# Products of a constant in front of the matrix products that a build-time order expects to find TensorE idle

## Chip, cores and metric

The kernel runs on one core of one Trainium2 chip. The metric is the device time of one execution in microseconds (us); three runs of the kernel before took 1369.7 to 1370.69, with a median of 1370.52.

## What is computed

Three layers follow one another. The first is attention with 2 batches, 8 heads, 576 positions and 64 columns per head, in which only the 32 largest scores of a row count. Its output, 1152 rows of 512 columns, goes through a mixture of 8 experts in which every expert sees every row and is weighted by a matrix that eight Sinkhorn sweeps balance. The result goes through a second mixture in which each row goes to its best expert, and at most 288 rows to one expert.

```python
scores = scale * np.matmul(q, k.transpose(0, 1, 3, 2))
mask = scores >= np.partition(scores, -32, axis=-1)[..., -32:-31]
attn = softmax(np.where(mask, scores, -1e9))
x = np.matmul(attn, v)                             # 1152 x 512
P = exp(x @ w_gate - max)                          # 8 sweeps over rows and columns
x2 = sum(P[:, e:e+1] * (np.maximum(x @ w1[e], 0) @ w2[e]) for e in range(8))
expert = np.argmax(x2 @ w_gate2, axis=1)           # at most 288 rows each
out[i] = gate[i] * (np.maximum(x2[i] @ w1b[e], 0) @ w2b[e])
```

## The kernel before

**Precision.** Each operand of a large product is split into a high and a low part of type fp32r (ScalarE rounds the high part, VectorE or GpSimd subtracts), and each product is three matrix products: high by high, high by low, low by high.

**The order.** The kernel does not issue instructions as its functions run. Each function describes jobs to an object of class `Order`: an engine, a rank, a cost in us, the jobs it depends on, the buffers it takes from pools and those it uses. When all is described, `run` takes, again and again, the job that can start first by these costs, and `put` calls its function, which emits its instructions. `self.t["PE"]` is the moment at which TensorE is done with what it has by this reckoning, and the start of the chosen job less that moment is the idle time that the order expects of TensorE. The order of the instructions on each engine is so fixed when the kernel is built; on the chip each engine works through its own list in that order, and waits on semaphores.

**Attention** (`keys`, `block`, `search`, `values`, L376 to L608). A block is 128 queries of one head. TensorE turns queries and keys (L214), forms the scores in two halves of 288 columns (L489) into PSUM, ScalarE copies them. VectorE finds the 32 largest in four rounds of MAX8 and MATCH_REPLACE8 (L504 to L510), masks the exponentials (L519). TensorE turns the result (L214), and after a pair's blocks multiplies it by the values in a chain of ten products (L596, here called a mix). ScalarE lifts one half of the mix (L599), and VectorE adds the other half (L601). PSUM tiles `tp` (a pool of three, `psa`) serve all of this.

**First mixture** (`mixture_one`, `late_one`, `visit`, `layer2`): products L693 and L717 into PSUM tiles `yp`, a pool of five (`psm`). The first group's attention, 16 blocks, must be done before the first of these products can start; the other groups' blocks are interleaved with them. **Sinkhorn** (L758 to L798) and the routing of rows (`route_all`, L906 to L976) follow: per tile of 128 rows, turn (L214), gate products (L928), choice on VectorE, count (L950, L951), place, and a scatter of the rows to HBM (L968).

**Second mixture** (`mixture_two`, L825 to L904). Per expert it fetches 288 rows (tile `x`) from HBM, turns them in 12 transposes of 96 rows (L214), three to a tile `tp`; ScalarE and VectorE split each tile (L851, L853), and eight units of products (L868: 12 products of 288 columns; L879: 12) follow. The transposes of the second expert come right behind those of the first, before its products. The end is the products of the last expert and the scatter of its rows (L898).

**What the change touches:** `Order.__init__`, `Order.run` (L114 to L127), `Net.build` (L218), the constant `ones_b` (L294, L295: 128 x 128 in bf16, written by GpSimd; so far used by the count alone), and the pool `psm`.

```python
s = max(self.t[j.eng], j.est)                    # Order.start: when a job could begin
...
self.t[e] = s + j.cost                           # Order.put: when its engine is done with it
...
self.psm = self.pool(ps, "yp", [128, 512], 5)    # Net.places
```

Of the kernel before, what the change touches and what calls it, by code (L numbers as in the profile page):

```python
# [36 lines left out]
class Pool:  # L37


    def __init__(self, tiles, line=True):  # L40
        self.free = [(0.0, t) for t in tiles]
        self.line, self.made, self.given = line, 0, 0
# [19 lines left out]
class Order:  # L62
# [9 lines left out]
    def __init__(self):  # L72
        self.t = {e: 0.0 for e in self.ENGINES}
        self.ready = {e: [] for e in self.ENGINES}
        self.left = 0
        self.moved = 0.0
        self.log = []

    def job(self, eng, rank, cost, fn, deps=(), take=(), use=(), est=0.0, lag=None):
# [33 lines left out]
    def run(self):  # L113
        while self.left:  # L114
            best = None
            for e in self.ENGINES:
                c = [(self.start(j), j.rank, n) for n, j in enumerate(self.ready[e])]
                c = [x for x in c if x[0] is not None]
                if not c:
                    continue  # L120
                s = min(c)[0]
                _, n = min((r, n) for t, r, n in c if t <= s + 0.02)
                if best is None or s < best[0]:
                    best = s, e, n
            assert best, "no job can start"
            self.put(*best)

    def put(self, s, e, n):
# [43 lines left out]
class Net:  # L172
# [45 lines left out]
    def build(self):  # L218
        with ExitStack() as st:
            self.st = st  # L220
            self.mem = self.space(st, "all")
            self.drams = self.space(st, "scratch", space=DRAM)
            self.places(st)
            self.constants()
            self.sa = ExitStack()
            self.places_a()
            self.attention()
            self.mixture_one()
            self.gate = self.job("X", 0, 0.0, self.turn_over, deps=self.attended)
            self.sinkhorn()  # L230
            self.late_one()
            self.mixture_two()
            self.o.run()
            self.sb.close()

    def places(self, st):
        ps = self.space(st, "psum", space=PSUM)
        self.psa = self.pool(ps, "tp", [128, 512], 3, line=False)
        self.psm = self.pool(ps, "yp", [128, 512], 5)
        w = self.mem  # L240
        self.r1 = self.pool(w, "ra", [128, 4, 128], 3)
        self.r2 = self.pool(w, "rb", [128, self.DM], 3)
        self.w1 = self.pairs(w, "w0", [128, 4, 128], 3)
        self.w2 = self.pairs(w, "w1", [128, self.DM], 4)
        self.h = self.pairs(w, "h", [128, 512], 3)
        self.ys = self.pool(w, "ys", [128, self.DM], 2)
        self.xt = [w.tile([128, 4, self.N], F32R, name=n) for n in ("xh", "xl")]
# [763 lines left out]
```

## Time and profile before

| | |
|---|---|
| time, median of 3 runs | 1370.52 us (1369.7 to 1370.69) |
| the profiled execution's own time | 1370.26 us |
| its span, first to last instruction | 1368.5 us |
| mean granted TensorE clock | 0.948 of full speed |
| TensorE busy | 1276.2 us, 93% |
| VectorE busy | 951.0 us, 69% |
| ScalarE busy | 794.5 us, 58% |
| GpSimd busy | 402.7 us, 29% |

PE is TensorE, PEld its loading of weights, DVE VectorE, ACT ScalarE, POOL GpSimd. A row of a timeline gives the start, the duration, the engine, the line of the code, the operation, output and inputs, their shapes and how many such instructions it merges; in brackets stand the idle time before it and who ended that. [...]

### The profile page before, as it was taken

The page shows a single profiled execution, that of the slowest core. Times are in us where ns is not written, and L with a number is a line of the kernel's source. Part 1 is how long each engine was busy: PE and PEld are TensorE (multiplying, and loading weights), DVE is VectorE, ACT ScalarE, POOL GpSimd, SP SyncE. Part 2 cuts the span into 40 slices and gives each one's busy share as a digit, 9 for nine tenths or more (in the row PEclk, how much of TensorE's full clock was granted, in tenths as well). Part 3 has the DMA queues.
Part 4 walks back from the last instruction along what each step waited for, and adds up shares of the span by engine and source line. Part 5 has one row for each costly group of instructions (what it writes and reads, how often), then busy time and mean ns, then how long its engine had stood idle before and what let it go on. Part 6 is the DMA issues. An engine that isn't in the chain of part 4 may idle for free. (4 is left out here: it accounts for less than half of the span.)

```text
span 1368.5 us, 22394 instructions
## 1 busy us (share of the span) xinstructions
PE 1276.2 (93%) x7315; PEld 1123.1 (82%) x7315; DVE 951.0 (69%) x2291; ACT 794.5 (58%) x1861; POOL 402.7 (29%) x414
## 2 busy tenths in 40 slices
PE   5567999999999999999979999999999978999997
PEld 3345878888899888888858888899988968999997
DVE  7998999999999999662564453555446744555652
ACT  6776878888898877433334333343334524655663
POOL 5633746787877743231000000000000010001001
PEclk9655899999999999999989999999999988999999
DMA  4500477465555523133673343444435634666661
GB/s 110 139 15 21 130 234 223 147 183 170 171 170 173 168 78 103 46 104 117 210 223 108 93 124 108 124 124 126 128 101 158 196 109 130 185 187 181 192 174 48
DMA packets 238213, 189.25 MB, mean 138 GB/s; under 512 B 44816, under 2 KB 188176, under 8 KB 238097
## 3 DMA queue, kind: packets, MB, share of 16 engines
q1 hardware_dynamic: 235840, 183.10, 45.9%
q0 software_dynamic: 2256, 4.73, 1.0%
q8 instruction: 57, 0.93, 0.3%
q14 instruction: 60, 0.48, 0.1%
HBM read 167.56 MB, written 22.57 MB: 139 GB/s over the span
## 5 line engine op out<-in xcount | busy, mean ns | idle before, releaser
L651 ACT ACTIVATE hh<-yp 128x256 fp32r<-128x256 f32 (+4 forms) x264 | 119.2, 451 | 253.8 <-PE yp L693 191.0
L653 DVE SCALAR_TENSOR_TENSOR hl<-yp,hh 128x256 fp32r<-128x256 f32 (+4 forms) x264 | 133.1, 504 | 188.8 <-ACT hh L651 188.4
L637 ACT ACTIVATE w1h<-rb 128x512 fp32r<-128x512 f32 x264 | 166.8, 632 | 155.3 <-PE yp L717 123.0
L717 PE MATMUL yp<-w1h,hh 128*128 128x512 f32 x552 | 222.8, 404 | 5.0 <-DVE acc L745 4.5
L717 PE MATMUL yp<-w1l,hh 128*128 128x512 f32 x552 | 218.1, 395 | 0.0
L717 PE MATMUL yp<-w1h,hl 128*128 128x512 f32 x552 | 217.8, 395 | 0.0
L640 DVE TENSOR_TENSOR w1l<-rb,w1h 128x512 fp32r<-128x512 f32 x160 | 110.6, 691 | 125.2 <-ACT w1h L637 125.1
L693 PE MATMUL yp<-xh,w0h 128*128 128x256 f32 (+3 forms) x832 | 175.0, 333 | 6.5 <-DVE acc L745 3.9
L693 PE MATMUL yp<-xh,w0l 128*128 128x256 f32 (+3 forms) x832 | 174.1, 331 | 0.0
L693 PE MATMUL yp<-xl,w0h 128*128 128x256 f32 (+3 forms) x832 | 173.5, 331 | 0.0
L637 ACT ACTIVATE w0h<-ra 128x512 fp32r<-128x512 f32 x272 | 169.8, 624 | 0.0
L643 POOL TENSOR_TENSOR w0l<-ra,w0h 128x512 fp32r<-128x512 f32 x104 | 134.8, 1296 | 110.9 <-ACT w0h L637 101.5
L693 PEld LDWEIGHTS yp<-xh,w0h 128*128 128x128 f32 x832 | 139.4, 191 | 28.3 <-DVE acc L745 4.6
L510 DVE MAX8 m<-wk 128x8 f32<-128x576 f32 x216 | 158.1, 745 | 0.4
L968 POOL DMA_INDIRECT disp<-acc,idx x9 | 10.1, 1118 | 488.5 <-DVE idx L964 488.5
L643 POOL TENSOR_TENSOR w1l<-rb,w1h 128x512 fp32r<-128x512 f32 x104 | 134.7, 1295 | 60.4 <-ACT w1h L637 56.5
L693 PEld LDWEIGHTS yp<-xh,w0l 128*128 128x128 f32 x832 | 135.7, 192 | 10.1 <-POOL w0l L643 0.5
L693 PEld LDWEIGHTS yp<-xl,w0h 128*128 128x128 f32 x832 | 135.8, 191 | 8.2 <-issue 0.2
L717 PEld LDWEIGHTS yp<-w1h,hl 128*128 128x128 f32 x552 | 104.3, 189 | 22.9
L717 PEld LDWEIGHTS yp<-w1h,hh 128*128 128x128 f32 x552 | 104.5, 189 | 21.7 <-DVE acc L745 4.5
L640 DVE TENSOR_TENSOR w0l<-ra,w0h 128x512 fp32r<-128x512 f32 x168 | 115.8, 689 | 5.2 <-ACT w0h L637 1.1
L717 PEld LDWEIGHTS yp<-w1l,hh 128*128 128x128 f32 x552 | 104.6, 190 | 14.0
(153 smaller groups left out, 2347.2 us busy)
## 6 DMA issues: line engine op xcount, KB each, us to landing
ra<-in_moe_w_dram SPq DMA_DIRECT2D x272, 256.0 KB, 2.9
rb<-in_moe_w_dram SPq DMA_DIRECT2D x272, 256.0 KB, 2.8
y<-ys SPq DMA_DIRECT2D x28, 256.0 KB, 3.0
disp<-z SPq DMA_DIRECT2D x1, 4626.0 KB, 16.3
x<-disp SPq DMA_DIRECT2D x8, 578.2 KB, 4.8
qg<-in_q_dram SPq DMA_DIRECT2D x64, 64.0 KB, 2.3
vr<-in_v_dram SPq DMA_DIRECT2D x32, 128.0 KB, 2.6
yt<-y SPq DMA_DIRECT2D x16, 256.0 KB, 3.6
```

The source lines that it names most:

```text
L510: j = self.job("DVE", r, 0.66, lambda i=i: nc.vector.max(m.t[:, i + 1], wk.t), deps=[j], use=[wk] if i == 2 else [])
L637: jh = self.job("ACT", -500 + rank, t_act(512, True), lambda r=r, w=w: nc.scalar.activation(w.t[0], r.t, AF.Copy), deps=[j], take=[w])
L640: jl = self.job("DVE", -100 + rank, t_dve(512, True), lambda r=r, w=w: nc.vector.tensor_sub(w.t[1], r.t, w.t[0].bitcast(F32)), deps=[jh], ...
L643: jl = self.job("POOL", -100 + rank, t_pool(512), lambda r=r, w=w: nc.gpsimd.tensor_sub(w.t[1], r.t, w.t[0].bitcast(F32)), deps=[jh], use=[r])
L651: jh = self.job("ACT", -1000 + k * 0.001, t_act(b - a), lambda: nc.scalar.activation(h.t[0][:, a:b], p.t[:, :b - a], AF.Relu), deps=deps, ...
L653: jl = self.job("DVE", -1000 + k * 0.001, t_dve(b - a), lambda: nc.vector.scalar_tensor_tensor(h.t[1][:, a:b], p.t[:, :b - a], 0.0, h.t[0] ...
L693: nc.tensor.matmul(p.t[:, :b - a], w1[0].t[i][:, d, :], self.xt[s][:, d, c0 + a:c0 + b], start=m == 0 and d == 0, stop=m == 2 and d == 3)
L717: nc.tensor.matmul(y[t].t, h.t[i][:, c:c + 128], w2[0].t[s], start=f == 0 and m == 0, stop=f == last and m == 2)
L968: i = nc.gpsimd.indirect_dma_start(out=self.disp, out_offset=bass.IndirectOffsetOnAxis(ap=v()["idx"][:, :1], axis=0), in_=x(), in_offset=N ...
```

## The change

`run` calls a hook each time the next job is one of TensorE's, with the idle time that the order expects before it. The hook, `Net.busy`, does nothing if that is under 1.0 us, or if no PSUM tile of the pool `psm` is free by the order's clock. Otherwise it emits, ahead of the job, as many products of `ones_b` by `ones_b` as fill 0.7 of the idle time at 0.23 us each. Each loads the 128 x 128 constant as weights, streams it four times (512 columns, bf16) and writes 128 x 512 into the free `yp` tile that has been free longest. Nobody reads the result: the next user of the tile starts its sum anew. The products are no jobs: the order's clock, ranks and buffers do not know of them, so the order of all other instructions stays as it was.

```diff
@@ class Order
         self.moved = 0.0
+        self.keep = None
         self.log = []
...
             assert best, "no job can start"
+            if best[1] == "PE" and self.keep:
+                self.keep(best[0] - self.t["PE"])
             self.put(*best)
@@ class Net, build
             self.st = st
+            self.o.keep = self.busy
...
+    def busy(self, idle):
+
+        free = [x for x in self.psm.free if x[0] <= self.o.t["PE"]]
+        if idle < 1.0 or not free:
+            return
+        b = self.ones_b
+        for _ in range(int(0.7 * idle / 0.23)):
+            self.nc.tensor.matmul(min(free, key=lambda x: x[0])[1], b, b[:, None, :].to_broadcast([128, 4, 128]),
+                                  start=True, stop=True)
```

## Rows read from the trace of the kernel before

**Rows 1.** The page: busy time by engine; TensorE and its granted clock in 40 slices.
```profile
PE 1276.2 (93%) x7315; PEld 1123.1 (82%) x7315; DVE 951.0 (69%) x2291; ACT 794.5 (58%) x1861; POOL 402.7 (29%) x414
...
PE   5567999999999999999979999999999978999997
...
PEclk9655899999999999999989999999999988999999
```

**Rows 2.** Busy time by stretch: length, then each engine, granted clock, DMA share, GB/s.
```profile
0.00:45.00 45.00, 26.37 (x90) 17.67 (x90) 34.26 (x90) 33.47 (x98) 24.91 (x47) 1.00 0.53 133
45.00:145.00 100.00, 65.33 (x236) 48.08 (x237) 89.00 (x242) 69.13 (x194) 43.38 (x61) 0.54 0.15 39
145.00:547.00 402.00, 394.78 (x2441) 344.48 (x2441) 395.60 (x1084) 338.38 (x866) 273.56 (x252) 0.99 0.56 166
...
1120.38:1140.86 20.48, 9.48 (x47) 8.65 (x47) 5.80 (x25) 3.68 (x10) 0.98 (x1) 0.50 0.31 78
...
1150.00:1340.00 190.00, 189.71 (x1472) 189.45 (x1471) 111.33 (x196) 111.97 (x236) 16.53 (x18) 1.00 0.64 181
```

**Rows 3.** TensorE's groups by form: scores in 0 to 42, then in 83 to 144.
```profile
L489 PE MATMUL tp<-kst,qs 128*128 128x288 f32 x30 | 10.8, 497 | 7.2 <-ACT kst L412 3.7 <-ACT sc L494 2.2 <-ACT er L552 1.1
...
L489 PE MATMUL tp<-kst,qs 128*128 128x288 f32 x29 | 10.4, 491 | 5.3 <-ACT er L552 4.8 <-ACT sc L494 0.5
```

**Rows 4.** Waits of VectorE, 45 to 145: us in total, times, longest.
```profile
DVE xr L601 <- ACT up L599: 8.1, 6, 2.3
```

**Rows 5.** Timeline of TensorE: the last mix of the first group; a mix later on.
```profile
133.68 0.58 PE L596 MATMUL tp<-eth,vs 128*128 128x256 f32 x1 [0.50 <-ACT sc L494]
...
136.07 0.41 PE L596 MATMUL tp<-etl,vs 64*128 64x256 f32 x1
...
330.88 0.28 PE L596 MATMUL tp<-eth,vs 128*128 128x256 f32 x1
...
332.14 0.28 PE L596 MATMUL tp<-etl,vs 64*128 64x256 f32 x1
```

**Rows 6.** Timeline of TensorE: neighbouring products of 512 columns, at 193 and at 704.
```profile
193.23 0.39 PE L717 MATMUL yp<-w1l,hh 128*128 128x512 f32 x1
193.46 0.40 PE L717 MATMUL yp<-w1h,hl 128*128 128x512 f32 x1
...
704.37 0.63 PE L717 MATMUL yp<-w1h,hl 128*128 128x512 f32 x1
704.80 0.63 PE L717 MATMUL yp<-w1h,hh 128*128 128x512 f32 x1
```

**Rows 7.** Timelines of GpSimd and of TensorE: the constant, the first transposes, those at 100.70.
```profile
1.17 0.20 POOL L295 MEMSET ones_b<- 128x128 bf16 x1
...
4.84 1.38 PE L214 MATMUL tp<-ident,kg 128*128 128x128 f32 x5 [4.84 <-DMA kg<-in_k_dram]
...
100.70 1.11 PE L214 MATMUL tp<-ident,e 128*128 128x128 f32 x4
```

**Rows 8.** Timeline of TensorE from the last routed tile into the second mixture.
```profile
1113.89 0.95 PE L928 MATMUL tp<-wg,xT 128*128 128x8 f32 x8
...
1119.00 0.66 PE L214 MATMUL tp<-ident,acc 128*128 128x128 f32 x4 [1.11 <-DVE acc L745]
1120.34 1.88 PE L928 MATMUL tp<-wg,xT 128*128 128x8 f32 x8 [0.69 <-ACT xT L923]
...
1133.39 4.21 PE L214 MATMUL tp<-ident,x 96*128 96x96 f32 x21 [9.73 <-DMA x<-disp]
1137.30 2.27 PE L868 MATMUL yp<-v,w0h 128*128 128x288 f32 x8
...
1140.86 1.22 PE L868 MATMUL yp<-v,w0h 128*128 128x288 f32 x8
```

**Rows 9.** Timeline of VectorE at the same place: the split of the turned rows.
```profile
1134.61 1.42 DVE L853 TENSOR_TENSOR v<-tp,v 128x288 fp32r<-128x288 f32 x3 [1.08 <-ACT v L851]
```

**Rows 10.** The chain that ended last: one unit's first layer at full clock.
```profile
1197.91 1.59 PE yp L868 x12
```

## The prediction

> **What bounds the kernel now.** I read the page first, then the busy times by stretch, then the waits, and only then single stretches of the timeline. The page shows TensorE busy for 93% of the span, and its granted clock near full except in a few slices: the first eighth, and a dip or two behind it [rows 1]. Clock is what this change can give, so those are the places to look at.
>
> By stretches [rows 2], the kernel has three kinds of time. From 145 on to 547 both TensorE (394.78 of 402 us) and VectorE (395.60) are full, at a clock of 0.99; there is no idle time to fill and no clock to win. Behind 1140.86 TensorE alone is the bound (189.71 of 190 us between 1150 and 1340), at full clock. What is left are two stretches at half clock. From 45 to 145 the mean is 0.54 while TensorE works 65.33 us of 100; VectorE with 89.00 is the bound, so TensorE's pace counts only where VectorE waits for it. From 1120.38 to 1140.86 it is 0.50, and TensorE works 9.48 of 20.48 us; here the second mixture starts, and every microsecond of TensorE is a microsecond of the end. For the first 45 us the view says 1.00, but there the clock has no record: the scores of 288 columns take 497 ns on average before 42, as the 491 of the stretch at 0.50 [rows 3]. So I count the first 42 us as half clock too.
>
> **How many products, and where.** The number is fixed by the costs in the code, not by the chip. Adding these up in the order of the jobs gives 37 places with an expected idle time of at least 1.0 us and a free tile, and 204 products: 30 places with 145 products ahead of the second group's attention (that is, before 145 us of the trace), three with 14 between 194 and 240, and four with 45 around the second mixture's start: 5 before the turn of the last routed tile, 4 before its count, 33 before the first transposes of expert 0 (expected idle 10.96 us; 0.7 x 10.96 / 0.23 = 33), 3 before those of expert 1. The waits beside the Sinkhorn sweeps get none, since all five `yp` tiles are taken. I use these expected times for the counts alone; durations come from the trace.
>
> **The price of one.** A bf16 product of 512 columns does not occur in this trace. The nearest are products of 512 columns in fp32r: 0.23 us from start to start at full clock, 0.43 at half [rows 6]. I take these two. So a burst fills 0.7 of the expected gap at full clock and 1.3 of it at half: at half clock the bursts are too long for their gaps, and the change rests on their raising the clock.
>
> **Part 1, the first 45 us.** The constant is written by 1.37 and the first transposes start at 4.84 [rows 7]. Eleven products at half clock take 4.7 us, to 6.1: these transposes come 1.3 us later, and VectorE waits for what follows. If the clock rises meanwhile, later transposes and scores get back about as much. Bounds: +1.3 and -1.5; I take +0.5.
>
> **Part 2, 45 to 145.** VectorE waits here for TensorE by way of the lifted half of the mixes: 8.1 us, six times, 2.3 at most [rows 4]. A mix takes 2.39 us from its first to its last start at half clock, 1.26 at full clock [rows 5]: 1.13 less. With all six at full clock this is 6.8 us at most, and VectorE, which is the bound, passes it on to the end. How many will be? The 145 products add between 33 us (full) and 62 us (half) to an engine that works 26 + 65 us of these 145, so the clock should be full for about half the time, as the bursts come and go: -3.4. Against it stand the bursts that find no gap. The transposes at 100.70 have no idle time before them [rows 7], yet get four products, 0.9 to 1.7 us; most other bursts fit at full clock. VectorE hides most of this; I charge +1.0. Part 2: -2.4, bounds -6.8 and +2.
>
> **Part 3, 194 to 240.** Fourteen products, 3.2 us at full clock, in a stretch in which VectorE and TensorE are both full [rows 2]. A short fall of the clock at 199 may vanish, but VectorE's work doesn't shrink: 0, bounds -1.5 and +1.
>
> **Part 4, the second mixture's start.** The five products fit the 1.11 us before the turn at 1119.00 (1.15). If the clock then holds over 1120.34, the eight gate products take 0.95 instead of 1.88 us [rows 8], on the path that ends in the scatter and the fetch of `x`: -0.9, bounds 0 and -0.9. The 33 take 7.6 us at full clock and lie in the 9.73 us in which TensorE waits for `x` [rows 8]. When `x` lands, 21 transposes go through three `tp` tiles before the first product of L868 can start, 3.91 us later. Halved they would save 1.9, but VectorE empties a tile per 0.47 us (three in 1.42) [rows 9], and the seventh tile needs the fourth one emptied; I take -0.7, and give back 0.25 for the three products between. Then the first unit: 3.56 us at half clock with three transposes in it, against 1.59 at full clock without them [rows 8, 10]. 12 products save 1.6, the transposes 0.2: -1.8. Part 4: -0.9 - 0.45 - 1.8 = -3.15, say -3.1.
>
> The burst ends some 2.7 us before `x` lands, and what comes next is transposes. The trace shows that 21 of them, back to back from 1133.39 for 4.2 us, did not raise the clock; it rose at 1140.86, after 3.5 us of products [rows 2, 8]. [...]
>
> **Sum.** +0.5 - 2.4 + 0 - 3.1 = -5.0 against the profiled execution's 1370.3 (0.3 below the median): **1365.3 us**, 0.4% less.
>
> **Rivals.** *The clock falls again between the burst and L868.* For it speak the 2.7 us of idle time and the transposes, which did not raise it before; against it, that a burst which begins at half clock ends later and leaves a smaller hole. +0.5 - 2.4 - 0.9 = -2.8: 1367.5.
>
> *Nothing comes of it.* The bursts in part 2 push as much as the faster mixes save, and the clock falls again in part 4; the gate's gain and the head's loss remain: 1370.3 + 0.5 - 0.9 = 1369.9. For it speaks that VectorE is the bound there and that nobody waits for most of TensorE's work.
>
> *Slower: products of a constant do not raise the clock.* The place is the burst of 33. At half clock it takes 33 x 0.43 = 14.2 us from 1123.66, to 1137.9; `x` is there at 1133.39, so all transposes come 4.5 us later, and the 1.3 at the head come on top: 1376.1. It decides at x us of half clock in the burst, with x/0.43 + (9.73 - x)/0.23 = 33, which is x = 4.6: if the clock rises before 1128.3, the burst still ends in time. Against it speaks that products raised the clock in 3.5 us at 1137.30, and nothing in the trace says that their values matter.
>
> **Numbers.** Forecast 0.42, clock falls 0.28, nothing 0.18, slower 0.12. A difference under 0.2%, 2.7 us, cannot be told from no change. The forecast is faster; the second case lies on that line (1367.8) and is split in halves; of the third a little is faster, the rest within. Faster 0.60, same 0.28, slower 0.12. The range: downward the forecast with part 2 near its bound (-6.8 instead of -2.4: 1360.9), upward the third case with the head's full 1.3, and some more for bursts without gaps: 1361.0 to 1371.5.
>
> **What would show it.** Right: a granted clock well above 0.54 from 45 to 145; VectorE's 8.1 us of waits for the lifted half near half of that; the stretch up to 145 shorter by 2 us; the gate products of the last tile at 0.95; the burst of 33 over before `x` lands, clock 1.00 behind it, the first L868 some 3.2 us after the landing. Wrong: a half clock again at the first L868 (second case); waits of VectorE that moved from L601 to another line (third); transposes of `x` that wait for the burst and not for the DMA (fourth). If products of bf16 take other than 0.23 and 0.43 us from start to start, every burst's length is wrong by that.

## The result, and the profile after

The kernel with the change took 1356.28 us (median of 4 runs, 1355.92 to 1360.54), the kernel before 1370.61 beside it: a ratio of 0.9904, interval 0.9883 to 0.9924 (ratios here and below are worked out from all runs of a set, so they are not the quotients of the medians). The profiled execution took 1356.15 us with a span of 1354.4, 14.1 less than before. The sign was forecast, the size was not: -14 instead of -5.0, and below the range.

One thing to keep in mind for all that follows: executions of one and the same kernel stand some us apart (the four of the change 4.6 us, at mean clocks of 0.977 to 0.982), and two traces of the change have a clock of 0.97 and of 0.88 from 45 to 145. So I read what a part is worth from traces, stretch by stretch, and use times for the verdict.

The page after (its first line and the lines of TensorE and its clock, as in [rows 1]):

```profile
PE 1293.3 (95%) x7519; PEld 1116.4 (82%) x7519; DVE 949.4 (70%) x2291; ACT 792.6 (59%) x1861; POOL 402.6 (30%) x414
...
PE   7777999999999999999979999999999999999997
...
PEclk8998999999999999899979999999999999999999
```

TensorE has 204 more instructions and 17 us more work. VectorE has the same 2291 instructions and the same work to 1.6 us. What changed is the clock in the first eighth (0.54 to 0.97 from 45 to 145, below), and the idle time of VectorE there. Busy times by stretch, to be laid beside [rows 2]:

```profile
0.00:45.00 45.00, 33.35 (x141) 18.22 (x141) 35.70 (x94) 34.68 (x103) 26.88 (x49) 0.89 0.56 142
45.00:145.00 100.00, 78.72 (x414) 50.33 (x413) 98.37 (x269) 77.46 (x219) 51.49 (x67) 0.97 0.21 55
145.00:547.00 402.00, 396.57 (x2445) 344.18 (x2444) 396.46 (x1086) 334.77 (x855) 266.89 (x247) 0.99 0.54 162
```

From 45 to 145 the granted clock is 0.97 instead of 0.54, and VectorE works 98.37 us of 100 instead of 89.00: its idle time fell from 11.0 to 1.6 us. The one row of its waits that is left, beside the 8.1 us of [rows 4]:

```profile
DVE xr L615 <- ACT up L613: 1.1, 1, 1.1
```

VectorE executes the same 2291 instructions in the same order in both traces, so each of its instructions has a start before and a start after, and their difference shows where time was won. The differences at some of them (my subtraction of starts in the two traces):

```
VectorE's instruction    start before   start after   difference
76  (MAX8)                      39.17         38.22        -0.96
335 (etl, L560)                147.58        135.26       -12.32
490                            203.44        191.04       -12.40
520                            215.69        201.25       -14.45
1400                           542.13        527.90       -14.22
1480                           587.87        575.18       -12.68
2040                          1115.79       1103.24       -12.55
2076 (hl, first unit)         1141.51       1127.35       -14.15
2290, the last                1355.97       1341.84       -14.13
```

Read downwards: -1.0 at the head, -11.4 between 39 and 148, nothing up to 203, -2.0 between 203 and 216, +1.5 given back between 542 and 588, -1.6 where the second mixture starts. Between 39 and 148 the waits for the lifted half (L601) shrank by 7.3 us and those for `e` and `etl` (L519, L560) by 2.7; the last 1.4 stand in no wait that the profile names.

The give-back is a dip of the clock that this execution has (0.50 from 541.76 to 545.17) and the profile of before did not have at that place (1.00 from 246.56 to 581.07). The busy times of two short stretches at half clock, after:

```profile
541.76:545.17 3.41, 3.41 (x11) 2.72 (x10) 2.63 (x7) 0.55 (x1) 0.00 (x0) 0.50 0.27 82
...
688.53:702.18 13.65, 7.14 (x18) 5.53 (x18) 7.88 (x11) 3.09 (x5) 0.85 (x1) 0.50 0.83 259
```

The first lies behind the eight-column gate products of the first mixture (538.66 to 541.39); the second is the wait beside the Sinkhorn sweeps, which got no bursts.

The start of the second mixture, after, in the timeline of TensorE (beside [rows 8]):

```profile
1105.17 1.25 PE L247 MATMUL yp<-ones_b 128*128 128x512 bf16 x5
1106.43 0.66 PE L217 MATMUL tp<-ident,acc 128*128 128x128 f32 x4
1107.78 1.06 PE L942 MATMUL tp<-wg,xT 128*128 128x8 f32 x8 [0.69 <-ACT xT L937]
...
1110.13 7.28 PE L247 MATMUL yp<-ones_b 128*128 128x512 bf16 x33
1120.03 0.96 PE L217 MATMUL tp<-ident,x 96*128 96x96 f32 x9 [2.62 <-DMA x<-disp]
1121.49 0.47 PE L217 MATMUL tp<-ident,x 96*128 96x96 f32 x3 [0.50 <-DVE v L867]
1121.80 1.26 PE L247 MATMUL yp<-ones_b 128*128 128x512 bf16 x3
1122.85 1.65 PE L217 MATMUL tp<-ident,x 96*128 96x96 f32 x9
1124.20 1.86 PE L882 MATMUL yp<-v,w0h 128*128 128x288 f32 x8
...
1126.71 1.22 PE L882 MATMUL yp<-v,w0h 128*128 128x288 f32 x8
```

The burst of 33 takes 7.28 us and is over 2.62 us before `x` lands: nobody waits for it. The gate products take 1.06 instead of 1.88 us. The first nine transposes take 0.96 us, at full clock (1.00 from 1108 to 1122). Then the clock falls: from 1122.02 to 1125.44 it is 0.50, and the second nine transposes (1.65 us) and the first half of the first unit run at half.

### The profile page after: what moved, and what is told of

The parts are those of the page before. It is cut to its first block, busy times and chain, and to the rows that moved or that the text cites. A ratio compares the mean times of both kernels' runs of the same rounds, so it can differ in the third digit from the quotient of the medians.

```text
span 1354.4 us, 22802 instructions
## 1 busy us (share of the span) xinstructions
PE 1293.3 (95%) x7519; PEld 1116.4 (82%) x7519; DVE 949.4 (70%) x2291; ACT 792.6 (59%) x1861; POOL 402.6 (30%) x414
## 5 line engine op out<-in xcount | busy, mean ns | idle before, releaser
L731 PEld LDWEIGHTS yp<-w1l,hh 128*128 128x128 f32 x552 | 104.7, 190 | 14.1
```

The costliest lines, as they stand in the source:

```text
L731: nc.tensor.matmul(y[t].t, h.t[i][:, c:c + 128], w2[0].t[s], start=f == 0 and m == 0, stop=f == last and m == 2)
```

## The experiments

My theory: TensorE's clock is what was won. A fuller clock shortens chains that VectorE waits for before 145 us, and there VectorE is the bound. Rivals: it is not the clock but the mere presence of instructions on TensorE; each part's bursts pay only together; the mixes alone explain it. The runs are called e1 to e14. Where a trace is read, "VectorE stands at -11.9" means that the named instruction of VectorE starts 11.9 us earlier than in the trace of before.

**Only the first 30 bursts, and only the last four.**

```diff
-        if idle < 1.0 or not free:
+        if idle < 1.0 or not free or self.o.t["PE"] > 150:     # e1
+        if idle < 1.0 or not free or self.o.t["PE"] < 1000:    # e2
```

> Only the 30 bursts (145 products) that the order places before its 150 us. If the gain is VectorE's waits in the first 150 us, which a fuller clock takes away: some 12.3 us less than before, so about 1358.2; the stretch from 194 to 240 and the start of the second mixture stay as they were (half clock behind the fetch of x). If the gain needed the later bursts as well (each part of the 14 us bought by its own bursts in equal measure of their number, 145 of 204): 10 us less, 1360.5.

> Only the four bursts (45 products) around the start of the second mixture. If parts add up: 1.6 us less than before by the aligned traces, up to 3.1 by the forecast's own sum, so 1367.4 to 1369.0, with the clock at half from 45 to 145 as before. If those bursts were worth what they cost (no gain): 1370.6.

e1: 1360.28 us, ratio 0.9908 (0.9891 to 0.9924). That is the rival's number, but the kernel before took 1372.0 beside it, 11.7 more, so the trace has to decide. VectorE stands at -11.9 at its instruction 335 and at -12.2 from 216 to 542, where the change has -14.2: the first stretch is bought by its own bursts, and the 2.0 us between 203 and 216 by the bursts at 194 to 240. At the second mixture nothing is won in e1 (-9.3 before, -9.2 behind), as expected without bursts there. Busy times of e1 from 45 to 145, and its fetch of `x`:

```profile
45.00:145.00 100.00, 79.16 (x410) 50.70 (x410) 97.80 (x267) 76.70 (x216) 50.83 (x67) 0.95 0.21 55
```

```profile
1124.10 4.21 PE L217 MATMUL tp<-ident,x 96*128 96x96 f32 x21 [9.92 <-DMA x<-disp]
1128.02 2.27 PE L882 MATMUL yp<-v,w0h 128*128 128x288 f32 x8
```

These are the durations of before [rows 8] to the digit. e2: 1371.8 us, ratio 0.9997 (0.9983 to 1.001). In its trace VectorE goes from +2.9 to +1.1 over the second mixture's start: 1.8 us are won there, about what the change won. By the times alone that could not be told from nothing, since its runs spread from 1366.5 to 1375.3.

**Is it the clock, or that instructions are there?** The same 204 products, of 8 columns instead of 512:

```diff
-            self.nc.tensor.matmul(min(free, key=lambda x: x[0])[1], b, b[:, None, :].to_broadcast([128, 4, 128]),
-                                  start=True, stop=True)
+            self.nc.tensor.matmul(min(free, key=lambda x: x[0])[1][:, :8], b, b[:, :8], start=True, stop=True)
```

> The same 204 places and the same number of products, but of 8 columns instead of 512, so that TensorE's list is as long and the array does almost nothing. If the gain is the clock: nothing is gained, 1370 to 1371.5, clock 0.54 from 45 to 145. If it is the mere presence of instructions in front of the waiting ones (an engine that is awake when the semaphore comes): the gain stays, 1356 to 1360.

1373.58 us, ratio 1.0006 (0.9987 to 1.0025). The clock from 45 to 145 is that of before, and so is VectorE's time:

```profile
45.00:145.00 100.00, 68.83 (x339) 54.26 (x340) 88.52 (x241) 68.42 (x193) 42.85 (x61) 0.53 0.15 39
```

Presence gains nothing here. The list of instructions is as long as with the change; what differs is that each product has 8 columns and not 512 (168 ns for one in the median, 379 with the change).

**Does it matter what is multiplied, or that it is a product?** First zeros in place of ones; then two fp32 transposes of a constant in place of each product.

```diff
-        b = self.ones_b
+        b = self.zero_b                     # e7, memset to 0.0
...
+            for _ in range(2):              # e3, in place of the matmul
+                self.tr(min(free, key=lambda x: x[0])[1][:, :128], self.ones)
```

> The same products of a constant that is zero instead of one. If only the engine's activity counts and not what it multiplies: as the change, 1356.3, clock 0.97 from 45 to 145. If the values matter for the clock (the rival that the forecast named): near or above before, 1370 to 1376.

> All 204 bursts' places, but each product is replaced by two transposes of 128 x 128 of a constant in fp32, which take the same 0.43 us at half clock and 0.22 at full clock. If transposes count for the clock as products do: the same gain, about 1356.5, clock 0.9 or more from 45 to 145. If they do not count: the clock stays near 0.54 there, the bursts are 1.3 times as long as their gaps, and the kernel is slower than before: 1372 to 1380 (4.5 us at the fetch of x, 1.3 at the head, and a few for the bursts between).

Zeros: 1356.66 us, ratio 0.9876 (0.9835 to 0.9917), clock 0.95 from 45 to 145. Zeros do as well as ones (1356.28 us, 0.97). Transposes: 1360.48 us, ratio 0.9913 (0.9883 to 0.9942). From 45 to 145:

```profile
45.00:145.00 100.00, 79.94 (x502) 64.87 (x500) 96.48 (x265) 75.16 (x211) 49.36 (x66) 0.91 0.19 49
```

0.91 is far from the 0.54 of before and the 0.53 of e4, so these transposes did raise the clock: that the 21 of [rows 8] had not, which spoke for the first rival, does not carry over to them. The time is 4 us above the 1356.5 that I expected for this case; whether that is the lower clock or the spread of single executions (the change itself has 0.88 in a second trace, below) is not shown. And behind 22 of them at the head, the kernel's own first transposes are fast. Timeline of e3:

```profile
1.60 4.93 PE L217 MATMUL yp<-ident,ones 128*128 128x128 f32 x22 [1.60 <-DVE ident L303]
6.32 0.93 PE L217 MATMUL tp<-ident,kg 128*128 128x128 f32 x5
```

These five take 0.93 us, 1.38 before [rows 7].

**How much is enough?** Bursts of 0.35 and of 1.0 of the expected gap.

```diff
-        for _ in range(int(0.7 * idle / 0.23)):
+        for _ in range(int(0.35 * idle / 0.23)):     # e5: 92 products
+        for _ in range(int(1.0 * idle / 0.23)):      # e6: 297 products
```

> Bursts that fill 0.35 of the expected gap instead of 0.7 (about half as many products). If the clock follows from TensorE's total work in a stretch: clock between the 0.54 of before and the 0.97 of the change from 45 to 145, about 0.75, and half of the gain: 1363 to 1364. If a little work is enough to hold it: 1357, as with all products.

> Bursts that fill the whole expected gap. The clock should be 0.97 or more from 45 to 145 and also behind the fetch of x (47 products at 0.22 us are 10.3 us, about the gap). If pushing costs more than the rest of the clock brings: 1357 to 1361, slower than the change. If the bursts stay hidden: 1355 to 1356.

e5: 1361.29 us, ratio 0.9907 (0.9874 to 0.9941); clock 0.62 from 45 to 145, and VectorE at -4.6 at its instruction 335. Half of the products did not hold the clock here, and the half dose got a third of that stretch's gain. What else it won lies in the small parts, which it got whole: 2.0 us between 203 and 216, 2.2 at the second mixture. e6: 1360.32 us, ratio 0.9908 (0.9874 to 0.9942). Its clock from 45 to 145 is 0.95, that of e1, but VectorE wins only 9.4 us up to 170 where e1 wins 12.0. Up to 2.6 us can be the price of the longer bursts (the second trace of the change, e9 below, wins 9.6 there, so one trace does not fix this number); it is seen best at the head, where the first transposes start at 6.93 instead of 4.84 [rows 7] and VectorE stands at +0.3 at 39. By the ratios neither dose can be told from the change (0.9904). Beside the zeros (e7), which ran in the same set from 1356.55 to 1357.22, both are slower in every run (e5 from 1358.96, e6 from 1358.63). Behind the fetch of `x` the full gap does better. Timeline of e6:

```profile
1113.57 10.30 PE L247 MATMUL yp<-ones_b 128*128 128x512 bf16 x47
1123.71 0.91 PE L217 MATMUL tp<-ident,x 96*128 96x96 f32 x9
...
1126.98 1.31 PE L882 MATMUL yp<-v,w0h 128*128 128x288 f32 x8
...
1128.92 1.20 PE L882 MATMUL yp<-v,w0h 128*128 128x288 f32 x8
```

47 products fill the gap, the clock holds (1.00 from 1123.7 to 1131), and the first unit starts 3.27 us after the first transpose and takes 1.94.

**Is it the mixes alone?** The kernel before without bursts, with five products instead of ten in each of the first group's eight mixes; all at half clock.

```diff
-                    for s in range(2):
+                    last = 1 if n > 15 else 0
+                    for s in range(last + 1):
```

> The kernel before, without any burst, in which the eight mixes of the first group leave out the products with the low part of the attention weights (five products instead of ten), all at half clock; the output's low bits are lost by that. If the gain before 145 us is the mixes' alone: VectorE is 11 us earlier at 145, as with the change. If the mixes give no more than their own shortening, 1.07 to 1.2 us each where VectorE waits for them (seven waits of 8.5 us in sum): 6 to 7 us earlier at 145, time 1364 to 1366, and the other 4 to 5 us of the change come from TensorE's work around the mixes.

1366.93 us, ratio 0.9967 (0.9945 to 0.9988); 3 us that it had won were lost between 542 and 588, where its trace, too, has a stretch at half clock (it starts between 537 and 557). Up to VectorE's instruction 335 it wins 8.3 us, 1.0 of them at the head (where the clock happened to be full from 12.2 to 15.6 without any burst): 7.3 us between 39 and 148, with the clock near that of before. Busy times and waits of VectorE from 45 to 145:

```profile
45.00:145.00 100.00, 65.69 (x252) 47.61 (x252) 95.60 (x261) 75.04 (x207) 48.21 (x65) 0.57 0.17 45
```

```profile
DVE xr L602 <- ACT up L600: 2.5, 3, 1.3
DVE etl L560 <- ACT eth L556: 1.2, 2, 0.8
```

So shorter mixes (1.0 to 1.2 us from first to last start) give about what I had set as the bound of a full clock, and by subtraction 4.1 of the change's 11.4 us come from TensorE's other work. Where that is can be seen at the last mix of the group. After the change, in the timeline of TensorE:

```profile
122.56 0.79 PE L503 MATMUL tp<-kst,qz 128*128 128x288 f32 x4 [0.52 <-ACT er L566]
124.11 0.39 PE L610 MATMUL tp<-eth,vs 128*128 128x256 f32 x1 [0.76 <-ACT sc L508]
...
125.47 0.28 PE L610 MATMUL tp<-etl,vs 64*128 64x256 f32 x1
```

and before:

```profile
131.85 1.33 PE L489 MATMUL tp<-kst,qz 128*128 128x288 f32 x4 [0.52 <-ACT er L552]
133.68 0.58 PE L596 MATMUL tp<-eth,vs 128*128 128x256 f32 x1 [0.50 <-ACT sc L494]
```

The mix itself takes 1.36 us from first to last start instead of 2.39, and the four scores in front of it, which TensorE must do first, 0.79 instead of 1.33. VectorE's wait behind them was 2.3 us and fell by 2.25: more than the 1.13 that I had allowed to a wait.

**Is the head's gain the bursts'?**

```diff
-        if idle < 1.0 or not free:
+        if idle < 1.0 or not free or self.o.t["PE"] < 6:
```

> The change without the three bursts (17 products) that the order places before its 6 us; 187 products are left. If the head's gain of 1.0 us is bought by these bursts raising the clock for the first scores: it is gone, VectorE stands at 0 to -0.3 against before at its 76th instruction, and the time is 1 us more than the change's, 1357 to 1357.5. If these bursts cost what the forecast charged (0.5, 1.3 at most): 0.5 to 1.3 us less than the change, about 1355.5.

1358.37 us, ratio 0.9902 (0.9866 to 0.9938). At VectorE's instruction 76 it stands at -0.9: neither the one nor the other. VectorE gets that far as fast without the 17 products as with them (30 later products before 45 us are left in). In the record of this execution the clock is full from 12.1 to 15.5, before any of its bursts, as it was in the run of the shorter mixes; in the traced execution of before it was not (its scores between 5 and 15 take 502 ns on average, here 438). The traces without these bursts stand at -0.3 (e2), -1.0 (e13) and -0.9 (e14), the two of the change at -1.0 and -0.4 (e9). So the -1.0 at the head cannot be put down to the change, and the 17 products there neither gain nor cost anything that I can show.

**The change again, and three versions meant to beat it.**

```diff
-        free = [x for x in self.psm.free if x[0] <= self.o.t["PE"]]
+        free = [x for x in self.psm.free + self.psa.free if x[0] <= self.o.t["PE"]]   # e8, e11, e12
-        if idle < 1.0 or not free:
+        if idle < 0.5 or not free:                                                    # e8, e10, e12
-        for _ in range(int(0.7 * idle / 0.23)):
+        for _ in range(int(0.9 * idle / 0.23)):                                       # e8
```

> A version meant to beat the change: bursts in expected gaps from 0.5 us on, 0.9 of each gap, and tiles of the pool tp as targets as well, so that the waits beside the Sinkhorn sweeps (688 to 702 at half clock in the trace of the change, some 6 us of products in it) are filled. If half clock at those places costs the end: 3 to 5 us less than the change, 1351 to 1353. If the sweeps' chain through VectorE sets the time there and bursts delay its matrix products and the writers of tp tiles: 1356 or more.

> The change itself, beside the three below on one chip. 1356 to 1358; the two dips of the clock behind 540 and the fall behind the fetch of x may stand elsewhere than in the first trace, which moves the time by 1 to 3 us.

> The change with bursts from 0.5 us of expected gap on instead of 1.0 (272 products: 198 + 23 + 51). If what is left before 145 us is the two stretches at half clock (16 to 26 and 108 to 115 in the trace of the change): both go, and 1.6 to 2 us with them, 1354.5 to 1355. If the short bursts push VectorE's chain more than that: 1356 or more.

> The change with tiles of the pool tp as targets too, from 1.0 us on (254 products: the 50 more lie beside the Sinkhorn sweeps). If the half clock there costs the end: the stretch of 10 to 14 us at half clock behind 688 is gone and 1.9 us with it (the difference between 1500 and 1700 of VectorE's list in the run with more bursts), 1354 to 1355. If the bursts delay the sweeps' own matrix products: no gain, 1356 or more.

> Both edits at 0.7 of the gap (326 products). If the two gains add up: 3.5 us less than the change, 1352 to 1353.5, and no slower than with 0.9 of the gap (1352.3), since less is pushed at the head. If filling 0.9 was what held the clock: 1354 or more.

```
run                             median us   runs from ... to     ratio to before (interval)   clock 45 to 145
e9   the change                   1356.51   1354.89 to 1362.59   0.9883 (0.9862 to 0.9905)    0.88
e10  gaps from 0.5 us             1353.72   1352.33 to 1356.43   0.9870 (0.9845 to 0.9895)    1.00
e11  tiles tp as well             1355.44   1355.41 to 1355.99   0.9880 (0.9859 to 0.9901)    0.95
e12  both, 0.7 of the gap         1354.49   1352.26 to 1355.78   0.9868 (0.9844 to 0.9892)    1.00
e8   both, 0.9 of the gap         1352.32   1349.82 to 1356.13   0.9837 (0.9795 to 0.9879)    1.00
```

The clock does what was expected: with bursts from 0.5 us on, neither e8 nor e10 has a stretch at half clock before 539 (1.00 from 45 to 145 in both), and VectorE stands at -13.8 instead of -12.3 at its instruction 335 in e10. With tiles of `tp` the half clock beside the Sinkhorn sweeps is gone: in the 15 us from 690 on the clock is 1.00 in e11 and 0.59 with the change, and VectorE wins 1.1 us there. The medians are 1 to 4 us below the change's, but the intervals overlap, and the gains do not add up in e12. I call none of them shown to be faster than the change; e8 is the best candidate, but it ran in another set (with e5 to e7), and its trace, the slowest of its four executions, loses 1.9 us beside the Sinkhorn sweeps at a clock of 1.00: the longer bursts may cost there what e11 gains.

e9 is a run of the change itself that says the same as the doses. Its traced execution was the slowest of its five, 1362.59 us, with a clock of 0.88 from 45 to 145:

```profile
45.00:145.00 100.00, 81.89 (x401) 52.36 (x399) 96.62 (x263) 75.36 (x211) 49.31 (x66) 0.88 0.19 49
```

VectorE won 7.6 us up to 137 there, 10.4 in the first trace. Same kernel, other clock, other time.

## Why the prediction was wrong

**What bounds the kernel** was read rightly: half clock before 145 (0.54 from 45 on) and behind the fetch of `x` (0.50), VectorE as the bound in the first stretch. That nothing can be won where both engines are full did not hold (part 3). The counts (145, 14 and 45 products) and the price of one (0.22 us from start to start at full clock, 7.28 us for 33; 0.23 forecast) held; the profile gives one of them 0.38 us, so neighbours overlap in it, as those of [rows 6] do.

The sign was right for the reason given, the clock. The size was not, and it would have been further off if part 4 had come out as forecast and if 1.5 us had not been lost behind 541.

**Part 2 failed, and it is the prediction's miss: -2.4 forecast, -11.4 measured.** Three terms of it were mis-sized, all the same way.

- *The clock would be full for about half the time.* It was 0.97 from 45 to 145. I took the share of time that the bursts add to and halved it, with no row that said what holds a clock. The doses show how steep this is: 65 of the 145 products gave 0.62, all 145 gave 0.88 to 0.97. And more in the large gaps (212 in e6) gave 0.95, while 198 that also lie in gaps from 0.5 us on gave 1.00 in e10 and e12: it seems that where they lie counts with how many they are.
- *6.8 us is the most that a full clock can save.* I allowed each wait of [rows 4] the shortening of the mix and nothing else. The run with shorter mixes shows that this was right for the mixes (7.3 us), but the waits behind them hold the scores in front as well, and other waits, for `e` and `etl`, gave 2.7 more: [rows 2] shows 11.0 us of idle time and not 8.1. The bound that needs no theory was that idle time, plus what follows up to 148. The lower end of the range, 1361.0, rested on the 6.8.
- *+1.0 for bursts without a gap.* At 0.7 of the gap nothing of it shows, nor at 0.9 (e8 stands at -14.0 at 170). At 1.0 of the gap it is up to 2.6 us.

**Part 3: 0 forecast, -2.0 measured.** I said that VectorE's work does not shrink. It doesn't, but it had idle time there, in the one wait that I did not look for because the stretch's total looked full. Timeline of VectorE before, and after at the same instruction:

```profile
206.73 0.42 DVE L653 SCALAR_TENSOR_TENSOR hl<-yp,hh 128x256 fp32r<-128x256 f32 x1 [1.40 <-ACT hh L651]
```

```profile
192.86 0.40 DVE L667 SCALAR_TENSOR_TENSOR hl<-yp,hh 128x256 fp32r<-128x256 f32 x1
```

The 1.40 us are gone, and with them most of the 2.0; two smaller waits up to 213 go as well. Without these bursts (e1) 1.22 us of this wait are left.

**Part 4: -3.1 forecast, -1.6 measured.** It came out between the forecast's case and the first rival. The gate gave 0.8 of the 0.9. Then the clock fell where that rival put it, but for 3.4 us only (0.50 from 1122.02 to 1125.44): the first unit started 4.17 us after `x` instead of 3.91 before (3.46 by the sum's -0.45; the 3.2 among the signs leaves out the three products between), and took 2.51 instead of 3.56 (1.8 forecast). Where the clock held, the working came out nearly right: with the gap filled (e6) the two terms are 3.27 and 1.94, and in e10, with the same burst of 33 (and six products more around the start of this mixture), they are 3.17 and 1.96, and VectorE wins 3.1 us between its instructions 2040 and 2076. Timeline of e10:

```profile
1107.89 7.28 PE L247 MATMUL yp<-ones_b 128*128 128x512 bf16 x33
1117.82 0.96 PE L217 MATMUL tp<-ident,x 96*128 96x96 f32 x9 [2.64 <-DMA x<-disp]
1118.62 0.60 PE L247 MATMUL yp<-ones_b 128*128 128x512 bf16 x2
...
1120.99 1.31 PE L882 MATMUL yp<-v,w0h 128*128 128x288 f32 x8
...
1122.95 1.22 PE L882 MATMUL yp<-v,w0h 128*128 128x288 f32 x8
```

The clock between the burst and the first unit was the open condition. The reason given with the rival, that the transposes of [rows 8] had not raised the clock before, does not carry over to e3, where transposes of 128 rows went with 0.91 from 45 to 145 (those of 96 were not tried). The hole behind the burst is not enough to explain the fall either: e10 has one of 2.64 us, as long as the 2.62 of the change, and the clock holds (the first eight products of L882 take 1.31 us, 1.86 with the change), while e12, with the same bursts here as e10 and a hole of 2.86 us, falls to 0.50 from 1117.94 to 1121.35. Why the clock falls in one and not in the other stays open.

**Part 1: +0.5 forecast, -1.0 measured**, inside its bounds. The cost was read rightly: the eleven products at half clock (4.72 us) end at 6.14, and the first transposes start at 5.98, 1.1 us later (1.3 forecast). That VectorE is early nevertheless cannot be put down to the bursts, by e13 and e14.

**The rivals.** "Products of a constant do not raise the clock" fell: ones and zeros raised it, by the same amount as far as these runs tell (0.54 before, 0.97 and 0.88 with ones, 0.95 with zeros). "Nothing comes of it" fell with part 2.

**What I did not see:** the dip of the clock behind 541 gave back 1.5 us. It is not the change's doing: all fifteen traces other than that of before have a stretch at half clock that starts between 537 and 557, those without bursts before 500 us (e2, e13) too, and VectorE loses 1.5 to 4.8 us there in all of them. The traced execution of before was a lucky one in this place (1.00 up to 581.07). And the half clock beside the Sinkhorn sweeps (0.50 from 703.95 to 714.19 before) is a third stretch that the forecast did not price; e11 wins 1.1 us there.

## What to carry to other kernels

Here TensorE's clock stood at 0.54 where TensorE worked 65 us of 100, and that was a cost to VectorE, which waited 8.1 us for the lifted halves of its mixes, though TensorE itself was far from the bound; products that nobody reads, in gaps that are known when the kernel is built, bought 1% here. Products of 8 columns in the same places did nothing (clock 0.53 there), half of the products got a third of the gain in the main stretch (0.62), and bursts as long as the whole expected gap held up the head (first transposes at 6.93 instead of 4.84). To bound such a gain, take the whole idle time of the engine that is the bound in the stretch, not the waits behind one kind of work. Where the clock differs from execution to execution, read each part's worth from traces aligned by an engine's own list of instructions; times of single executions spread by more than most of the parts are worth (7.7 us in e9), and one trace of each kernel is not enough for the small ones.

## What the runs showed of the hardware that was not expected

- fp32 transposes of 128 x 128, issued as products with the identity, raised TensorE's clock in e3: 0.91 from 45 to 145 with 290 of them ahead of 145 us in place of 145 products (0.54 before, 0.88 to 0.97 with products). Why 21 transposes of 96 rows [rows 8] did not raise the clock before (0.50 from 1133.39 to 1137.30) stays open.
- Products of zeros held it as well as products of ones: 0.95 from 45 to 145, against 0.97 and 0.88 in the two traces of the change with ones.
- The clock differs from execution to execution of one kernel: the change itself ran from 1354.89 to 1362.59 us in one set of five, at mean clocks of 0.983 and 0.975.
